# Six of the last z-gradient blocks brought token-major by a transposing load instead of by TensorE

## Chip, cores, metric

One core of a Trainium2 chip runs the whole program. The metric is the device time of one execution in microseconds (us). Three executions of the kernel before were timed; their median is the number that the kernel after is compared with. A fourth one, profiled, gives the trace.

## What is computed

The reference is the forward pass and the gradient of two alternating blocks, each used twice on a sequence of 2048 tokens with 512 columns. A is a long convolution (q times a filtered product of k and v), B is a dense layer with GELU. What matters here is the gradient of B's weights, summed over its two uses (layers 3 and 1):

```python
def _B_ref(x, w1, b1, w2, b2):
    h = jnp.einsum("bsd,df->bsf", x, w1) + b1
    h = _gelu(h)
    return jnp.einsum("bsf,fd->bsd", h, w2) + b2
```

With z the input of the GELU and gz its gradient (2048 tokens by F = 1376), the gradient of w1 is x^T gz (512 by 1376) and that of b1 is the sum of gz over the tokens. Both are summed over the two layers. The gradient of w2 is h^T g, with g the gradient that comes into the block.

## The kernel before

F is cut into NFC = 11 blocks of 128 columns (the last has 96). `weight_grads` (L1980) goes through 44 **units**, listed by `weight_grad_units` (L1970): a unit is one block c of one layer i. Units 0 to 21 (`which` = 0) make the gradient of w2 from h, units 22 to 43 (`which` = 1) that of w1 from gz. From unit 26 on the two layers of a block are neighbours: an even unit and the odd one after it sum into one PSUM tile `dw_ps`. Units 42 and 43 are the 96-column block.

A unit needs its 128 by 2048 block **token-major** (tokens on the partitions) as 16 weights of 128 by 128 in a tile `dw_tm`. Units 0 to 21 get it by a transposing load from DRAM (L2005). Units 22 to 43 load it feature-major (`dw_fm`, L2008), four units ahead; `turn_half` (L2010) then turns it on TensorE in two halves: eight transposes against the identity into one PSUM tile `dw_tp` (two buffers, shared with `dw_pt`), which ScalarE (ACT) copies to `dw_tm` (L2020). The halves of unit k+1 are issued in unit k before products 2 and 9. In unit 41, which has two successors in the tail, unit 43's halves come before products 5 and 13 (L2105).

`sum_rows` (L2023) sums the feature-major tile over the tokens for b1, then gives the tile back. It runs on ACT (L2027) while `m.sum_on_act` is set, else on VectorE (DVE, L2029). It stands before product 12 of unit k for unit k+1. `turn_out` (L2032) turns a finished block (`dw_pt`) in the second unit after it, `flush` (L2053) stores it.

The tail (L2077 to L2097) is the 96-column block. It goes the other way round: for each of four column blocks `dc`, 32 products of 96 columns (16 per layer), then an ACT copy (L2095) and a store of 192-byte rows. Before the third column block `sum_out` (L2042) turns the b1 sums.

Tiles come from seven tags; `take` (L1991) hands out the one that has been free longest, `give` returns one. A load on the SP queue into a tag waits for the tag's last reader, and everything behind it on SP waits too.

**Order of the work.** `weight_grads` is a generator that fills the gaps of `conv_backward` (the gradient of A): the latter yields the time it can spare, and products are issued until that is used up. A product counts 0.23, a half turn 0.45. TensorE, DVE and SP keep this program order. The stages of `conv_backward` from unit 33 on are, for each of four column blocks `cc`, 57 products `gh_ps` whose PSUM tiles (two buffers) ACT copies to `Wh` (L1265, L1269), then vector work, and between the second and the third 16 rows of `gk_ps`. Each `gh` stage yields 7.0:

```python
            yield 7.0
            state.sum_on_act = False
            if cc == 1:
                yield from k_rows()
```

so that sums go to ACT until the first `gh` stage has been covered. When `conv_backward` is through, the rest of the generator runs on its own. By these numbers and by the trace, the first `gh` stage lies in unit 33, the second in unit 34, the third in unit 38, the fourth in unit 39; what is left after that is unit 40, unit 41 and the tail.

Of the kernel before, what the change touches and what calls it, by code (L numbers as in the profile page):

```python
# [1349 lines left out]
def tok(ap2d, s):  # L1350
    return ap2d[s * 512:(s + 1) * 512, :].rearrange("(t p) d -> p t d", p=P)
# [625 lines left out]
    return units  # L1977


def weight_grads(nc, m, dims, aps, d):  # L1980


    D, F, S, ND, NFC, NT = dims.D, dims.F, dims.S, dims.ND, dims.NFC, dims.NT
    out7, out8, out9, out10 = aps["out_7"], aps["out_8"], aps["out_9"], aps["out_10"]
    b1a = d.evp.tile([P, 2, NFC], F32, name="b1a", tag="b1a", bufs=1)
    layers = (3, 1)
    units = weight_grad_units(NFC)
    fms, tms, pss, turned, late = {}, {}, {}, [], []
    spare, held = [f"dw_t{x}" for x in (0, 1, 2, 4, 5, 3, 6)], {}

    def take(name, key):  # L1991
        tag = held[key] = spare.pop(0)
        pool = d.evp if tag in ("dw_t3", "dw_t6") else d.tp if tag == "dw_t5" else d.share
        return pool.tile([P, S], BF16, name=name, tag=tag, bufs=1)

    def give(key):
        spare.append(held.pop(key))

    def fetch(k, sync):
        if k >= len(units):  # L2000
            return
        which, i, c = units[k]
        if which == 0:
            tms[k] = take("dw_tm", ("tm", k))[:, :].rearrange("p (t f) -> p t f", t=NT)
            sync.dma_start_transpose(out=tms[k], in_=m.h_d[layers[i]][:, c, :])  # L2005
        else:
            fms[k] = take("dw_fm", ("fm", k))
            sync.dma_start(out=fms[k], in_=m.gz_d[layers[i]][:, c, :])  # L2008

    def turn_half(k, half):  # L2010
        if k >= len(units) or not units[k][0]:
            return 0.0
        if half == 0:
            tms[k] = take("dw_tm", ("tm", k))[:, :].rearrange("p (t f) -> p t f", t=NT)
        ps = d.pp.tile([P, 8, P], BF16, name="dw_tp", tag="dw_tp")
        for j in range(8):
            t = 8 * half + j
            nc.tensor.transpose(out=ps[:, j, :], in_=fms[k][:, t * P:(t + 1) * P], identity=m.ident)
        dst = tms[k][:, 8 * half:8 * half + 8, :]
        nc.scalar.activation(out=dst, in_=ps, func=ACT.Identity)  # L2020
        return 0.45

    def sum_rows(k):  # L2023
        if k < len(units) and units[k][0]:
            which, i, c = units[k]
            if m.sum_on_act:
                nc.scalar.activation(out=fms[k], in_=fms[k], func=ACT.Identity, accum_out=b1a[:, i, c:c + 1])  # L2027
            else:
                nc.vector.tensor_reduce(out=b1a[:, i, c:c + 1], in_=fms[k], op=ALU.add, axis=mybir.AxisListType.X)  # L2029
            give(("fm", k))  # L2030

    def turn_out():  # L2032
        for o, f0, fcs in turned:
            pt = d.pp.tile([P, ND, P], F32, name="dw_pt", tag="dw_tp")
            for dc in range(ND):
                nc.tensor.matmul(pt[:, dc, :], lhsT=o[:, dc * P:(dc + 1) * P], rhs=m.ident, start=True, stop=True)
            oT = d.evp.tile([P, ND, P], BF16, name="dw_oT", tag="dw_oT")
            nc.scalar.activation(out=oT, in_=pt, func=ACT.Identity)
            late.append((oT[:, :, 0:fcs], out7[:, f0:f0 + fcs].rearrange("(c p) f -> p c f", p=P)))
        turned.clear()  # L2040

    def sum_out():  # L2042
        b1o = d.evp.tile([P, NFC], BF16, name="b1o", tag="b1o", bufs=1)
        nc.vector.tensor_tensor(out=b1o, in0=b1a[:, 0, :], in1=b1a[:, 1, :], op=ALU.add)
        pb = d.pp.tile([NFC, P], BF16, name="b1_ps", tag="dw_tp")
        nc.tensor.transpose(out=pb, in_=b1o, identity=m.ident)
        b1r = d.evp.tile([NFC, P], BF16, name="b1r", tag="b1r", bufs=1)
        nc.vector.tensor_copy(out=b1r, in_=pb)
        nfull = F // P
        late.append((b1r[0:nfull, :], out8[0:nfull * P].rearrange("(c p) -> c p", p=P)))  # L2050
        late.append((b1r[nfull:NFC, 0:F - nfull * P], out8[nfull * P:F].rearrange("(o p) -> o p", o=1)))

    def flush():  # L2053
        for o, ap in late:
            nc.sync.dma_start(out=ap, in_=o)
        late.clear()

    def reload(x, l):
        for s in range(4):
            nc.sync.dma_start(out=m.G[x][:, s * TS:(s + 1) * TS, :], in_=tok(m.n_d[l], s))  # L2060

    for k in m.early:
        held["tm", k] = spare.pop(0)
        tms[k] = m.early[k]
    fetched = 5
    for k in range(len(m.early), fetched):
        fetch(k, nc.sync)
    yield 0.01
    last = []
    for k, (which, i, c) in enumerate(units):  # L2070
        if which == 1 and units[k - 1][0] == 0:
            reload(1, 1)
        while fetched < len(units) and fetched <= k + (4 if units[fetched][0] else 5):
            fetch(fetched, nc.sync)
            fetched += 1
        f0, fcs = dims.FC[c]
        if which and c == NFC - 1:  # L2077
            last.append(tms.pop(k))
            if i == 0:
                continue  # L2080
            ps = d.pp.tile([P, ND, P], F32, name="dw_ps", tag="dw_ps")
            o = d.evp.tile([P, ND, P], BF16, name="dw_oT", tag="dw_oT")
            for dc in range(ND):
                for i in range(2):
                    for t in range(NT):
                        if (dc, i, t) == (0, 0, 7):
                            turn_out()
                        if (dc, i, t) == (2, 0, 0):
                            sum_out()
                        if (dc, i, t) == (3, 0, 0):  # L2090
                            flush()
                        nc.tensor.matmul(ps[:, dc, 0:fcs], lhsT=m.G[i][:, t, dc * P:(dc + 1) * P], rhs=last[i][:, t, 0:fcs],
                                         start=(i == 0 and t == 0), stop=(i == 1 and t == NT - 1))
                        yield 0.05
                nc.scalar.activation(out=o[:, dc, 0:fcs], in_=ps[:, dc, 0:fcs], func=ACT.Identity)  # L2095
                nc.sync.dma_start(out=out7[dc * P:(dc + 1) * P, f0:f0 + fcs], in_=o[:, dc, 0:fcs])
            continue  # L2097
        if i == 0:
            pss[c] = d.pp.tile([P, D], F32, name="dw_ps", tag="dw_tp" if which == 0 and c in (2, 3) else "dw_ps")
        ps, tm = pss[c], tms.pop(k)  # L2100
        for t in range(NT):
            if t in (2, 9):
                if turn_half(k + 1, int(t == 9)):
                    yield 0.45
            if k == len(units) - 3 and t in (5, 13):  # L2105
                yield turn_half(k + 2, int(t == 13))
            if t == 7:
                turn_out()
            if t == 12:
                flush()  # L2110
                sum_rows(k + 1)
            if k == len(units) - 3 and t == 15:
                sum_rows(k + 2)
            nc.tensor.matmul(ps, lhsT=tm[:, t, :], rhs=m.G[i][:, t, :], start=(i == 0 and t == 0),
                             stop=(i == 1 and t == NT - 1))
            yield 0.23
        give(("tm", k))
        if which == 0 and i == 0 and c == NFC - 1:
            reload(0, 3)
        if i == 0:  # L2120
            continue
        o = d.evp.tile([P, D], BF16, name="dw_o", tag="dw_o")
        nc.scalar.activation(out=o, in_=ps, func=ACT.Identity)  # L2123
        if which == 0:
            late.append((o[0:fcs, :], out9[f0:f0 + fcs, :]))
            if c == NFC - 1:
                b2o = d.evp.tile([P, D], BF16, name="b2o", tag="b2o", bufs=2)[fcs:fcs + 1, :]
                nc.scalar.activation(out=b2o, in_=ps[fcs:fcs + 1, :], func=ACT.Identity, scale=1.0 / PAD_H)
                late.append((b2o, out10.rearrange("(o d) -> o d", o=1)))
        else:  # L2130
            turned.append((o, f0, fcs))
    turn_out()
    flush()
# [301 lines left out]
```

## Time and profile before

| | us |
|---|---|
| median of 3 runs | 780.03 (779.84 to 780.92) |
| the profiled execution | 779.15 |
| its span, from first to last instruction | 776.9 |
| TensorE (PE) busy in the span | 743.0 (96%) |
| VectorE (DVE) busy | 705.6 (91%) |
| ScalarE (ACT) busy | 584.7 (75%) |
| GpSimd (POOL) busy | 222.8 (29%) |

The profiled execution takes 2.25 us more than its span, for what lies before the first and after the last instruction. In the trace's rows a matmul is one of TensorE's instructions and its weight load (PEld) another; line 56 is a helper through which every ordered instruction is recorded, so tiles tell them apart. In brackets stands the idle time before a row and what ended it.

### The profile page before, as it was taken

What the parts mean: (1) busy time and instruction counts of PE and PEld (TensorE: products, weight loads), DVE (VectorE), ACT (ScalarE), POOL (GpSimd) and SP (SyncE); (2) the same over time, 40 slices, a digit from 0 to 9 for tenths busy, and PEclk for the clock granted to TensorE, in tenths of its full rate; (3) what the DMA queues carried; (4) which work ended last, traced back from release to release, by engine and by line L of the source; (5) the groups of instructions that cost most, each with busy time, mean ns of one, the idle gap of its engine ahead of it and who ended that gap; (6) DMA issues with size and microseconds to landing.
All of it is one profiled execution on the core that took longest, in us unless ns stands there. A gap on an engine that the chain in (4) does not pass through costs nothing. (4 is left out here: it accounts for less than half of the span.)

```text
span 776.9 us, 13847 instructions
## 1 busy us (share of the span) xinstructions
PE 743.0 (96%) x5263; PEld 457.3 (59%) x5263; DVE 705.6 (91%) x1146; ACT 584.7 (75%) x792; POOL 222.8 (29%) x308
## 2 busy tenths in 40 slices
PE   8999899989999999999999999989999999999994
PEld 6765345655666666766666566434444465567764
DVE  8997999999999999999999989975999999999381
ACT  6999887799999999999788855445232199976662
POOL 6534520011233455254443342310012133020100
PEclk9999999999999999999999999999999999999998
DMA  9978888635571555779787978999999997755321
GB/s 313 332 287 308 298 317 293 119 89 136 161 215 49 168 144 167 209 206 216 217 249 205 254 181 239 235 312 248 255 269 193 375 390 278 252 154 170 116 76 26
DMA packets 199288, 169.39 MB, mean 218 GB/s; under 512 B 94195, under 2 KB 178870, under 8 KB 199094
## 3 DMA queue, kind: packets, MB, share of 16 engines
q1 hardware_dynamic: 186006, 127.31, 59.0%
q0 software_dynamic: 13216, 41.20, 15.1%
q8 instruction: 41, 0.67, 0.4%
q14 instruction: 25, 0.20, 0.1%
HBM read 76.36 MB, written 76.36 MB: 197 GB/s over the span
## 5 line engine op out<-in xcount | busy, mean ns | idle before, releaser
L56 PEld LDWEIGHTS <-w_sb 128*128 128x128 bf16 x903 | 84.9, 98 | 35.4 <-DMA low<-low 4.6
L56 PEld LDWEIGHTS <-dw_tm 128*128 128x128 bf16 x672 | 62.8, 98 | 64.0 <-DMA dw_tm<-h_d 2.4
L56 PE MATMUL mm_ps<-low,w_sb 128*128 128x256 bf16 x660 | 86.8, 273 | 3.9 <-DMA low<-low 3.9
L56 PE MATMUL dw_ps<-G,dw_tm 128*128 128x512 bf16 x336 | 82.6, 379 | 2.0 <-DMA dw_tm<-h_d 1.9
L56 PE MATMUL dw_ps<-x_sl,dw_tm 128*128 128x512 bf16 x336 | 81.8, 379 | 0.0
L56 PEld LDWEIGHTS <-w2T_sb 128*128 128x128 bf16 x704 | 68.9, 98 | 16.4 <-issue 1.0
L56 POOL TENSOR_TENSOR rstd<-rstd,mhalf 128x2 f32<-128x2 f32 (+1 forms) x28 | 36.3, 1296 | 98.0 <-DVE rstd L56 96.7
L56 PE MATMUL mm_ps<-W,w2T_sb 128*128 128x256 bf16 x440 | 58.3, 272 | 0.5 <-ACT l_g L56 0.3
L56 ACT ACTIVATE l_g<-l_g 128x2816 bf16<-128x2816 bf16 x22 | 57.2, 2601 | 1.4 <-DVE l_g L56 1.3
L56 POOL TENSOR_SCALAR ibx<-ident,ib 128x128 bf16<-128x128 bf16 x32 | 33.3, 1044 | 84.6 <-DVE W L56 82.2
L2020 ACT ACTIVATE dw_tm<-dw_tp 128x1024 bf16<-128x1024 bf16 x44 | 45.0, 1024 | 13.9 <-PE dw_tp L56 13.1
L2123 ACT ACTIVATE dw_o<-dw_ps 128x512 bf16<-128x512 f32 x21 | 12.5, 594 | 42.7 <-PE dw_ps L56 30.9
L56 PEld LDWEIGHTS <-ib 128*128 128x128 bf16 x264 | 25.6, 98 | 27.9 <-DVE ib L56 1.0
L56 DVE SCALAR_TENSOR_TENSOR gw_junk<-gy_bf,kTc 128x1024 bf16<-128x1024 bf16 x32 | 39.2, 1225 | 2.2 <-ACT gy_bf L1176 1.1
L56 ACT ACTIVATE l_n<-l_n,ib 128x512 bf16<-128x512 bf16 x32 | 25.5, 827 | 13.3 <-POOL ib L56 8.2
L56 PE MATMUL oo_ps<-w1T_sb,ib 128*128 128x512 bf16 x154 | 35.0, 379 | 0.0
L56 PE MATMUL mm_ps<-lane_t,w2T_sb 128*128 128x256 bf16 x264 | 34.0, 273 | 0.0
L56 ACT ACTIVATE W<-W 128x2816 bf16<-128x2816 bf16 x12 | 31.7, 2642 | 0.0
L56 ACT ACTIVATE low<-x_sl,nmr,rstd 128x512 bf16<-128x512 bf16 x36 | 30.2, 870 | 1.8 <-DVE nmr L56 1.8
L56 PE MATMUL oo_ps<-w_sb,l_h 128*128 128x512 bf16 x132 | 30.5, 379 | 0.5 <-DVE l_h L56 0.5
L56 ACT ACTIVATE ibx<-mm_ps 128x512 bf16<-128x512 f32 (+1 forms) x36 | 20.2, 577 | 14.2 <-PE mm_ps L56 14.1
L56 DVE TENSOR_TENSOR l_g<-l_g,l_g 128x2816 bf16<-128x2816 bf16 x19 | 30.7, 1614 | 0.0
(381 smaller groups left out, 1960.6 us busy)
## 6 DMA issues: line engine op xcount, KB each, us to landing
dw_fm<-gz_d SPq DMA_DIRECT2D x22, 512.0 KB, 10.7
l_n<-n_d SPq DMA_DIRECT2D x26, 256.0 KB, 3.7
gz_d<-ib SPq DMA_DIRECT2D x7, 704.0 KB, 5.1
W<-gp_d SPq DMA_DIRECT2D x7, 704.0 KB, 6.5
n_d<-low SPq DMA_DIRECT2D x18, 256.0 KB, 2.6
h_d<-l_h SPq DMA_DIRECT2D x6, 704.0 KB, 5.4
gz_d<-ibx SPq DMA_DIRECT2D x6, 704.0 KB, 4.8
KVspec_d<-KVg SPq DMA_DIRECT2D x4, 1024.0 KB, 6.4
```

What stands on the lines that cost most here:

```text
L56: return self.tc.keep_in_program_order(f(*args, **kwargs))
L2020: nc.scalar.activation(out=dst, in_=ps, func=ACT.Identity)
L2123: nc.scalar.activation(out=o, in_=ps, func=ACT.Identity)
```

## The change

Units 34, 36, 38, 40, 42 and 43 get their token-major tile by a transposing load from DRAM, issued on SP at the start of the unit three before, right after the feature-major load of the unit four ahead. They are not turned on TensorE and not copied by ACT. Their feature-major tile is still loaded, for the b1 sum; that sum is issued one unit earlier than it was, so that two sums stand together in units 32, 34, 36, 38 and 40, and unit 43's stands in unit 41 before product 12.

```diff
+TURNED_BY_LOAD = (34, 36, 38, 40, 42, 43)
...
+    def fetch_turned(k, sync):
+        if k in TURNED_BY_LOAD:
+            which, i, c = units[k]
+            tms[k] = take("dw_tm", ("tm", k))[:, :].rearrange("p (t f) -> p t f", t=NT)
+            sync.dma_start_transpose(out=tms[k], in_=m.gz_d[layers[i]][:, c, :])
+
     def turn_half(k, half):
-        if k >= len(units) or not units[k][0]:
+        if k >= len(units) or not units[k][0] or k in TURNED_BY_LOAD:
             return 0.0
...
             fetched += 1
+        fetch_turned(k + 3, nc.sync)
...
             if k == len(units) - 3 and t in (5, 13):
-                yield turn_half(k + 2, int(t == 13))
+                if turn_half(k + 2, int(t == 13)):
+                    yield 0.45
...
                 flush()
-                sum_rows(k + 1)
-            if k == len(units) - 3 and t == 15:
+                if k + 1 not in TURNED_BY_LOAD:
+                    sum_rows(k + 1)
+                if k + 2 in TURNED_BY_LOAD:
+                    sum_rows(k + 2)
+            if k == len(units) - 3 and t == 15 and k + 2 not in TURNED_BY_LOAD:
                 sum_rows(k + 2)
```

## Rows read from the trace of the kernel before

**Rows 1.** The page: busy us, share, instructions by engine; the instruction queue's packets, MB, share.

```profile
PE 743.0 (96%) x5263; PEld 457.3 (59%) x5263; DVE 705.6 (91%) x1146; ACT 584.7 (75%) x792; POOL 222.8 (29%) x308
...
q8 instruction: 41, 0.67, 0.4%
```

**Rows 2.** Stretches of the span: busy us (instructions) of PE, PEld, DVE, ACT, POOL; granted clock, DMA share, GB/s.

```profile
680.00:700.00 20.00, 18.47 (x153) 13.45 (x151) 19.29 (x30) 14.99 (x27) 4.11 (x3) 1.00 0.52 152
...
765.00:771.00 6.00, 0.37 (x9) 0.26 (x7) 0.00 (x0) 0.01 (x1) 0.00 (x0) 0.93 0.00 0
771.00:775.00 4.00, 2.72 (x32) 2.50 (x31) 0.00 (x0) 0.49 (x2) 0.00 (x0) 0.50 0.19 40
```

**Rows 3.** The chain of work that ended last, two pieces: start, us, what.

```profile
702.49 0.45 PE dw_tp L56 x8
...
763.80 7.17 another core or an unknown queue
```

**Rows 4.** The instructions in order of time, 677 to 696 us, ACT and TensorE.

```profile
677.73 1.90 ACT L2027 ACTIVATE dw_fm<-dw_fm 128x2048 bf16<-128x2048 bf16 x1
...
679.76 1.02 ACT L2020 ACTIVATE dw_tm<-dw_tp 128x1024 bf16<-128x1024 bf16 x1
680.68 1.09 ACT L1265 ACTIVATE Wh<-gh_ps 128x514 bf16<-128x514 f32 x2
681.33 5.50 PE L56 MATMUL gh_ps<-tabG,GY 128*128 128x257 bf16 x48 [1.18 <-ACT Wh L1265]
...
689.75 1.90 ACT L2027 ACTIVATE dw_fm<-dw_fm 128x2048 bf16<-128x2048 bf16 x1
...
691.64 0.59 ACT L2123 ACTIVATE dw_o<-dw_ps 128x512 bf16<-128x512 f32 x1
...
692.28 0.23 PEld L56 LDWEIGHTS <-dw_o 128*128 128x128 bf16 x4 [0.52 <-ACT dw_o L2123]
...
693.84 1.02 ACT L2020 ACTIVATE dw_tm<-dw_tp 128x1024 bf16<-128x1024 bf16 x1 [0.21 <-PE dw_tp L56]
694.07 0.38 PE L56 MATMUL gh_ps<-tabG,GY 128*128 128x257 bf16 x2
...
695.47 4.74 PE L56 MATMUL gh_ps<-tabG,GY 128*128 128x257 bf16 x41 [0.25 <-ACT Wh L1265]
```

**Rows 5.** The token-major tile: the transposing loads' issue time on SP in ns; landing in us.

```profile
L56 SPq DMA_TRANSPOSE dw_tm<-h_d x22: 2065/4222/12769, 478.6 to 598.1; - x22
...
DMA to landing us min/median/max: 4.6/7.5/10.1
```

**Rows 6.** The instructions in order of time, the tail from 759 us, TensorE and one ACT copy.

```profile
759.07 0.46 PE L56 MATMUL dw_ps<-dw_tm,G 128*128 128x96 bf16 x7
760.19 0.40 PE L56 MATMUL dw_pt<-ident,dw_o 128*128 128x128 bf16 x4 [0.66 <-ACT dw_o L2123]
...
763.85 0.84 PE L56 MATMUL dw_ps<-dw_tm,G 128*128 128x96 bf16 x16 [0.19 <-ACT dw_oT L2095]
764.52 0.84 PE L56 MATMUL dw_ps<-dw_tm,x_sl 128*128 128x96 bf16 x16
...
770.99 0.25 ACT L2095 ACTIVATE dw_oT<-dw_ps 128x96 bf16<-128x96 f32 x1 [7.19 <-remote]
...
771.29 1.44 PE L56 MATMUL dw_ps<-dw_tm,G 128*128 128x96 bf16 x16 [5.92 <-ACT dw_oT L2095]
772.53 1.48 PE L56 MATMUL dw_ps<-dw_tm,x_sl 128*128 128x96 bf16 x16
```

**Rows 7.** The DMA queues from 762 to 768 us: packets, MB, share of 16 engines.

```profile
DMA packets 289, 0.07 MB, mean 11 GB/s; under 512 B 288, under 2 KB 288, under 8 KB 288
...
q8 instruction: 1, 0.02, 3.1%
```

**Rows 8.** The waits, 8 to 757 us: us in total, times, longest.

```profile
PE mm_ps L56 <- DMA low<-low: 3.9, 2, 2.3
```

**Rows 9.** The last stores of the convolution's gradient, POOL, in order of time.

```profile
755.75 0.53 POOL L1287 DMA_DIRECT2D out_dram<-gh  x1 [13.21 <-DVE gdo L56]
```

## The prediction

> **What bounds the kernel.** I read the page first: TensorE is busy for 96% of the span, DVE for 91%, ACT for 75% [rows 1]. Next the stretches: from 680 us on TensorE still has 18.5 of 20 us, while the DMA engines are down to half their time [rows 2]. So work taken off TensorE there is worth its time, and DMA has room to take it. The chain of waits then shows two things that the shares hide. It runs through the turned halves, at 0.45 us a piece [rows 3], and it ends in 7.17 us "another core or an unknown queue". The timeline of the tail shows what that is: TensorE finishes the third column block at 765.36, its release reaches ACT only at 770.99, and TensorE starts again at 771.29 after 5.92 us without work [rows 6]. The timeline from 677 to 696 us shows that ACT is the second bound here: TensorE waits for ACT's `Wh` copies 1.18 us in the first `gh` stage and 0.25 us in the second, and 0.52 us for `dw_o` in unit 34, each behind a sum of the b1 gradient or the copy of a turned half [rows 4].
>
> **The sum, part by part.** (1) *Turning.* Six units have 12 halves; at 0.45 us [rows 3] TensorE loses 5.4 us of work. All of it is on the path: the `gh` stages lie at fixed amounts of counted work, a half (0.45) being replaced there by two products (0.46), so the saving shows after the fourth `gh` stage, where unit 40, unit 41 and the tail shrink to 7 products, unit 41 and the tail. -5.4.
>
> (2) *Waits behind unit 34's sum.* Now 1.90 us of ACT at 689.75 stand ahead of `dw_o` [rows 4]. That sum moves to unit 32, so the wait of 0.52 goes. -0.5.
>
> (3) *First `gh` stage.* In unit 32 two sums (33 and 34) now follow each other on ACT. Ahead of the first `Wh` copy a sum, one slot of 2.03 us (677.73 to 679.76), takes the place of a copy, one slot of 0.92 (679.76 to 680.68) [rows 4]. TensorE's wait of 1.18 grows to 2.3. +1.1.
>
> (4) *Second `gh` stage.* Here the change costs most. Sums 35 and 36 both come before product 12 of unit 34. By the counted work the first `gh` stage's 7.0 is not yet used up there (13 products of unit 33, then 12 products and two halves of unit 34, at 0.23 and 0.45, make 6.65), so both go to ACT, where before 35 went to DVE. TensorE reaches the stage at 694.07, plus 1.1 and less 0.9 for the two halves of 34, less 0.5 of (2), plus 0.7 for three more products: about 694.4. Two groups take it 1.15 us (694.07 to 695.22), to 695.6. ACT copies unit 35's second half (at about 693.5, 0.92), then makes two sums of 1.95 (2.03 and 1.89 in the rows), and only then copies `Wh`, 0.65 until TensorE resumes: 699.0 [rows 4]. A wait of 3.4 us in place of 0.25. Bounds: 0 if ACT took the copy first, 4.1 if both sums count in full. I take +3.1, by the row of the first stage, where ACT kept exactly this order.
>
> (5) *Start of the tail.* `dw_o` no longer queues behind unit 43's copy; of the 0.66 us wait [rows 6] I take off 0.2.
>
> (6) *The loads.* Six transposing loads of 512 KB are new. They landed in 7.5 us, 10.1 at most, and held SP 2.1 to 12.8 us each [rows 5]. Every one has three units of work ahead of its use, more than 13 us; the shortest is 43's, which waits on SP for unit 38's last product and is used after units 39, 40, 41 and the fourth `gh` stage (48 products at 0.23, two halves, 57 products at 5.50/48 = 0.115 [rows 4]): 18.5 us. Worst case by the rows is 12.8 + 10.1 = 22.9, late by 4.4; the median leaves 11. I take 0. Behind a waiting load on SP stand feature-major loads, due a unit or more later, and stores that nothing reads. DVE's sums 39 and 40 now wait for their loads and push the second `gh` stage's vector work back a few us; its result goes to a store only. The last such store was issued at 755.75 [rows 9]; it moves to about 759 and lands long before the end. Sums 41 to 43 now stand ahead of the last vector work, so `sum_out` waits for no sum.
>
> So far -5.4 - 0.5 + 1.1 + 3.1 - 0.2 = -1.9 us.
>
> The Trainium skill (VectorE: DVE Perf Modes, Rules for kernel authors) speaks against the change: turn 128 by 128 on TensorE where PSUM will do, at 390 ns against 1309 ns by DMA. An estimate from that page is 16 blocks x 1.309 = 21 us a unit, which would bring 43 late by some 2.5 us. The rows have 7.5 us for all 16 blocks and the measurement decides.
>
> (7) *The 5.92 us hole in the tail* is larger than all this. 41 packets of the instruction queue serve 10,526 TensorE instructions [rows 1], about 257 each (an estimate). One of them moves just before the hole [rows 7], and it is slow: 3.1% of 16 engines in 6 us is 3.0 us, against 0.4% of 16 x 776.9 us / 41 = 1.2 us in the mean [rows 1]. It moves among two stores of 192-byte rows, 288 packets under 512 bytes [rows 7]. In the tail a product takes under 50 ns (32 in 1.51 us, 763.85 to 765.36 [rows 6]), so whatever is late in instructions shows there and is covered elsewhere. The change removes 12 x 8 x 2 = 192 instructions, three quarters of a packet. Only 64 follow the hole, so the last call falls beyond the end, and the call before it comes to lie 257 - 192 = 65 instructions ahead of the old place: between the second and the third column block, its packet moving while the first block is computed, before any of those small stores. Bounds: the hole stays (0, and 1.2 more, since the third block too would run at the half clock that followed the hole: granted 0.50, 1.2 of 2.4 GHz, after 771 [rows 2], 2.72 us for a block in place of 1.51 [rows 6]); or it goes, -5.6 (a usual wait for ACT of some 0.3 remains) and -1.2. Forty other packets left no hole in the chain, and this one's company is gone, so I take the second.
>
> The Trainium skill (Runtime: NRT & Kernel Launch, Instruction fetch mechanics) says that the next block is fetched while the current one runs and that a crossing is mostly hidden. By that rule the hole is an exception and the time is the forecast's; by the row as it stands, it is the first rival's.
>
> **Total.** 776.9 - 1.9 - 5.6 - 1.2 = 768.2 us of span. The profiled execution took 779.15, 2.25 more than its span, and the median is another 0.88 above: **771.4 us**.
>
> **Rivals.** *The hole stays, one block earlier:* 776.9 - 1.9 + 1.2, on the median 779.4. For it: the tail's pace is the same, and that a fetch is the cause is inferred from one packet. Against it: the packet's slowness goes with its neighbours.
> *Slower: the wait for the two sums costs the clock.* TensorE's longest earlier wait was 2.3 us [rows 8] and cost none; 5.9 us did [rows 2, 6]. The new wait of 3.4 lies between. If the clock falls, the 48 products left of that `gh` stage take twice 0.115: +5.5. With the hole in place that is 784.9, without it 776.9; so it decides the sign if the hole stays.
> *ACT does not hold TensorE,* because sums and copies go another way round: parts (3) and (4) cost nothing and the sum is -6.1: 767.2, or 775 with the hole.
> *Loads come late* (the bounds of (6)): 43 by 4.4 us, 775.8, or 783.8 with the hole. The page on VectorE named under (6) would lead here too.
> *The change does nothing* would need the halves to be off the path; the chain names them.
>
> **Chances.** Forecast 0.48; hole stays 0.29; clock lost 0.08; ACT holds nothing 0.07; loads late 0.08. The range runs from 768.8 to 780.8: it takes the forecast, the first rival and the mixed cases, and leaves out the slow ends and the best one. The forecast's own range is 769 to 774. A measurement here can tell about 0.2%, 1.6 us. Faster: 0.48 + 0.07 + half of clock and loads + a little of the first rival, 0.62. Within it: most of the first rival, 0.25. Slower: 0.13.
>
> **What would show it.** Right: 256 of the 22 x 16 transposes left and 32 copies of turned halves; TensorE idle about 3.4 us at the second `gh` stage, released by `Wh`, behind two sums; the chain without an unknown piece, the tail's four column blocks about 1.9 us apart, the clock at 1.00 to the end. Wrong: an idle of 5 us between the second and third column block (first rival); a wait of TensorE or DVE for `dw_tm<-gz_d` or `dw_fm`; a granted clock under 1.00 near 697 us.

## The result and the profile after

The change made the kernel slower: 793.6 us median of six runs, against 782.0 for the kernel before beside it, a ratio on record of 1.0137 (95% interval 1.0104 to 1.0171; the two medians divided give 1.0149). The forecast was 771.4, with 768.8 to 780.8 as its range. The profiled execution took 791.14 us, its span 789.1, against 779.15 and 776.9 before.

The first view is the page: the engines' busy time, and the instruction queue. They answer to [rows 1].

```profile
PE 736.0 (93%) x5089; PEld 452.9 (57%) x5167; DVE 702.3 (89%) x1144; ACT 576.7 (73%) x784; POOL 221.6 (28%) x308
...
q8 instruction: 40, 0.66, 0.3%
```

The work did go: TensorE has 96 weight loads fewer, 12 halves of 8 (5263 to 5167; some matmul records are missing after, so the loads are counted), and its busy time fell. Its share fell too, so it waits more than before. Where, is best seen by cutting the span at marks that both kernels have. Each time is read from the timeline or the chain:

| stretch | before | after | difference | forecast |
|---|---|---|---|---|
| start to the first copy of a turned half (code that is the same) | 619.7 | 623.0 | +3.3 | 0 |
| to the 48 products of the first `gh` stage | 61.6 | 70.7 | +9.0 | +1.1 |
| to those of the fourth `gh` stage | 62.2 | 62.9 | +0.8 | +2.6 |
| to the last row of products | 29.0 | 17.1 | -11.9 | -11.8 |
| to the end of the span | 4.4 | 15.4 | +11.0 | -0.6 |
| sum | 776.9 | 789.1 | +12.2 | -8.7 |

The forecast's column sorts its own steps into these stretches: (3); (2) and (4); (1), (5), the hole of (7) and 0.6 of its 1.2 for the half clock (the hole's last block began in the fourth stretch); the other 0.6. The fourth row came as forecast, the second and the last cost 20 us between them. (The first row is not put down to the change: over the thirteen kernels profiled for this text that mark lies between 619.7 and 629.8.)

**The second row** is in ACT's part of the timeline, and in TensorE's beside it (start, us, instruction; in brackets the idle time before it and what ended it):

```profile
677.06 1.91 ACT L2036 ACTIVATE dw_fm<-dw_fm 128x2048 bf16<-128x2048 bf16 x1 [6.52 <-DMA dw_fm<-gz_d]
...
678.97 1.01 ACT L2029 ACTIVATE dw_tm<-dw_tp 128x1024 bf16<-128x1024 bf16 x1
```

```profile
680.03 0.61 PE L56 MATMUL dw_ps<-x_sl,dw_tm 128*128 128x512 bf16 x1 [5.63 <-ACT dw_tm L2029]
...
693.67 5.50 PE L56 MATMUL gh_ps<-tabG,GY 128*128 128x257 bf16 x48 [2.02 <-ACT Wh L1265]
...
708.32 5.50 PE L56 MATMUL gh_ps<-tabG,GY 128*128 128x257 bf16 x48 [1.21 <-ACT Wh L1265]
```

ACT stood 6.52 us at a sum of b1 whose feature-major tile was not there yet. That is unit 34's sum, and it had been put ahead of the copy of unit 31's second half, two units before its own place. TensorE then waited 5.63 us for that copy, with the tile's transposed blocks long done. The chain (start, us, what) names the load, 14.14 us from issue to landing, and the stretch behind it, shown last, ran at half clock:

```profile
662.90 14.14 DMA dw_fm<-gz_d
677.06 2.00 ACT dw_fm L2036 x2
```

```profile
679.00:686.00 7.00, 5.75 (x26) 3.23 (x28) 6.79 (x14) 7.00 (x9) 0.00 (x0) 0.51 0.35 75
```

(The last three numbers of a stretch are the granted clock, the DMA share and GB/s: 0.51 is the 1.2 GHz level.) The wait of 5.63, half of the 5.9 us that TensorE worked at that level (680.03 to 685.9) and the `gh` wait that grew from 1.18 to 2.02 [rows 4] make 9.4, a little over the stretch's 9.0.

**The last rows** are in the tail's timeline, which answers to [rows 6], POOL's stores, which answer to [rows 9], SP's waits (us in total, times, longest) and the DMA issues from 758 to 775 us (KB, median us to landing). An issue whose landing the trace doesn't tell is left out of the median; the last line is the issue of 771.16 by itself:

```profile
769.32 0.84 PE L56 MATMUL dw_ps<-dw_tm,G 128*128 128x96 bf16 x16 [0.34 <-ACT dw_oT L2105]
...
771.18 0.84 PE L56 MATMUL dw_ps<-dw_tm,G 128*128 128x96 bf16 x16 [0.19 <-ACT dw_oT L2105]
...
773.04 0.84 PE L56 MATMUL dw_ps<-dw_tm,G 128*128 128x96 bf16 x16 [0.34 <-ACT dw_oT L2105]
773.72 0.84 PE L56 MATMUL dw_ps<-dw_tm,x_sl 128*128 128x96 bf16 x16
```

```profile
769.50 0.53 POOL L1287 DMA_DIRECT2D out_dram<-gh  x1 [13.94 <-DVE b1o L56]
770.02 0.76 POOL L1289 DMA_DIRECT2D out_dram<-gdo  x1
```

```profile
SPq L2444 <- DMA out_dram<-gdo: 10.3, 1, 10.3
```

```profile
out_dram<-dw_oT SPq DMA_DIRECT2D x4, 24.0 KB, 14.3
out_dram<-gdo POOLq DMA_DIRECT2D x1, 1.0 KB, 16.6
...
out_dram<-dw_oT SPq DMA_DIRECT2D x1, 24.0 KB, 15.9
```

The hole is gone: four column blocks 1.86 us apart, where before one lay behind 5.92 us of nothing. But the kernel no longer ends with them. It ends with `gdo`, 512 sums of 2 bytes each, stored one element at a time (L1289). It is issued at 770.02 and lands 16.6 us later, at 786.6, when TensorE has been done for 12 us. The 24 KB store issued 0.7 us ahead of it (769.30) lands in 1.6 us; those issued behind it, at 771.16 and 773.01, need 15.9 and 14.3 us and land just after it. Before, `gdo` went out at 756.28, right behind the store of [rows 9]. The store issued at 761.96 needed 11.6 us, the one at 774.32 again 1.5, and their median is

```profile
out_dram<-dw_oT SPq DMA_DIRECT2D x4, 24.0 KB, 6.6
```

The views of the kernel before give no landing for `gdo`; the last mark of it in the trace is at 772.88, again 16.6 us after the issue.

### The profile page after: what moved, and what is told of

Its sections match the earlier page's. It is cut to its first block, busy times and chain, and to the rows that moved or that the text cites. A ratio compares the mean times of both kernels' runs of the same rounds, so it can differ in the third digit from the quotient of the medians.

```text
span 789.1 us, 13570 instructions
## 1 busy us (share of the span) xinstructions
PE 736.0 (93%) x5089; PEld 452.9 (57%) x5167; DVE 702.3 (89%) x1144; ACT 576.7 (73%) x784; POOL 221.6 (28%) x308
## 5 line engine op out<-in xcount | busy, mean ns | idle before, releaser
L56 PE MATMUL dw_ps<-x_sl,dw_tm 128*128 128x512 bf16 x325 | 79.7, 384 | 6.5 <-ACT dw_tm L2029 5.6
L56 PE MATMUL dw_ps<-G,dw_tm 128*128 128x512 bf16 x321 | 80.5, 381 | 2.5 <-DMA dw_tm<-h_d 1.8
L2029 ACT ACTIVATE dw_tm<-dw_tp 128x1024 bf16<-128x1024 bf16 x32 | 32.6, 1023 | 6.0 <-PE dw_tp L56 5.5
L56 DVE TENSOR_REDUCE b1a<-dw_fm 128x1 f32<-128x2048 bf16 x10 | 22.6, 2279 | 9.4 <-DMA dw_fm<-gz_d 9.4
```

Of the source, the lines that this page charges most:

```text
L56: return self.tc.keep_in_program_order(f(*args, **kwargs))
```

## The experiments

All stand against the kernel before, run on the same chip in turn; where no interval is given, the kernel ran once. Two theories came from this profile. *The order:* ACT's sum runs too early because nothing holds it. *The store:* the scattered `gdo` needs some 16 us and slows what is issued behind it; after, it sets the end, and before, it made the hole. Its rival is the forecast's reading, that the hole hangs on where an instruction packet falls.

**ACT in the written order.** The Ordered wrapper, which keeps an engine's instructions in the order of the text, covered TensorE, DVE and SP for the weight gradients, not ACT.

```diff
-            fill = weight_grads(Ordered(nc, tc, ("tensor", "vector", "sync")), m, dims, aps, dw)
+            fill = weight_grads(Ordered(nc, tc, ("tensor", "vector", "scalar", "sync")), m, dims, aps, dw)
```

> The kernel after, with ACT's instructions of the weight gradients kept in the order in which they are written, so that unit 34's sum stays behind unit 31's second copy. If the moved sum is what stops TensorE in unit 31, the idle of 5.6 us before unit 31's product 8 and the 6.8 us at half clock behind it (3.4 us lost) go, and the ratio to the kernel before falls from 1.014 to about 1.003 (some 9 us less than after). If the idle there is the load's own lateness (the rival), the sum still holds ACT for some us, now in unit 32, and less than 4 us is gained. Either way the end still waits for the store of the column sums gdo: TensorE's last product to the end of the span 12 us or more, as in the kernel after.

Measured: 785.05 us, ratio 1.006 (1.0038 to 1.0082). The stall in unit 31 is gone, with its half clock, and ACT waits for no feature-major tile any more, so the load was in time for the sum's own place. The `gh` stages then show what the forecast had worked out for this order (TensorE's timeline; then the stretch behind the second wait, its clock third from the right):

```profile
684.15 5.51 PE L56 MATMUL gh_ps<-tabG,GY 128*128 128x257 bf16 x48 [2.02 <-ACT Wh L1265]
...
700.69 7.14 PE L56 MATMUL gh_ps<-tabG,GY 128*128 128x257 bf16 x48 [3.10 <-ACT Wh L1265]
```

```profile
701.00:704.00 3.00, 3.00 (x17) 2.10 (x16) 3.00 (x6) 0.74 (x3) 0.60 (x1) 0.51 1.53 198
```

Waits of 2.02 and 3.10 us, forecast 2.3 and 3.4; and after the 3.10 the clock fell, which made the 48 products 7.14 us long in place of 5.50. So some 6 us were gained, not 9: in the kernel after, a sum that ran early no longer stood ahead of the second stage (1.21 us there), and in order it does: that stretch of the table is 66.4 us here, 3.5 more than after. The end is as it was, 13 us behind TensorE (SP's waits at the end):

```profile
SPq L2444 <- DMA out_dram<-gdo: 10.1, 1, 10.1
```

**`gdo` as four rows of 256 bytes,** in the kernel after, in the kernel before, and with ACT in order:

```diff
-            dma(out=out6.rearrange("(c p) -> p c", p=P), in_=gdo)
+        pg = d.pp.tile([ND, P], BF16, name="gdo_ps", tag="dw_tp")
+        nc.tensor.transpose(out=pg, in_=m.gdo, identity=m.ident)
+        gdr = d.evp.tile([ND, P], BF16, name="gdr", tag="gdr", bufs=1)
+        nc.scalar.activation(out=gdr, in_=pg, func=ACT.Identity)
+        nc.sync.dma_start(out=aps["out_6"].rearrange("(c p) -> c p", p=P), in_=gdr)
```

> The kernel after, with gdo turned on TensorE (two instructions) and stored by SP as 4 rows of 256 bytes in place of 512 elements of 2 bytes. If the scattered store is what ends the span and slows the other small stores, the last store lands within 4 us of TensorE's last product and the ratio falls from 1.014 to about 1.000 (some 10 to 11 us less). If small stores are slow by themselves at that point (the rival), the end stays 10 us or more behind TensorE's last product and the ratio at 1.01 or above. The stall of unit 31 stays, 5.6 us.

> The kernel before, with the same edit of gdo's store and nothing else. Theory: the scattered store, issued at 756 us, is what makes the 5.92 us hole between the third and fourth column block, by slowing the transfers around it (an instruction packet among them): the hole goes, ratio about 0.991 (7 us less). Rival, the prediction's: the hole belongs to the place of an instruction packet, 64 instructions before the end, which two more instructions hardly move: the hole stays at some 5 us, ratio 0.997 to 1.002.

> The kernel after with both edits. If the two causes are apart and both as supposed, their gains add up: ratio about 0.988 (9 us less in unit 31, 10 to 11 us less at the end, against a kernel after at 1.014), which would be below the kernel before and a little below the kernel before with gdo's rows (0.991). If only one holds, the ratio is that of its own run.

Measured: 1.0048 (1.0029 to 1.0068) after, 0.9969 (0.994 to 0.9998) before, 0.9987 (0.9967 to 1.0006) with ACT in order. In each the span ends within 4 us of TensorE's last product, and in the kernel before the hole is gone (0.34 us in its place); but each fell short of its number (1.000, 0.991 and 0.988). The list of waits gives a reason: one of 4.5 us that the kernel before has at 0.9, in code that was not touched (all three have this row). The third also has the wait of 3.10 us in the second `gh` stage, and its 48 products took 8.28 us.

```profile
PE iv_ps L56 <- DVE Yb L56: 4.5, 1, 4.5
```

The new tag `gdr` takes memory, so other tiles can move, and a DVE copy at 538 to 540 us (`spec_rb`), which had no wait in the kernel before, waits 12.2 us for TensorE, where the kernel before waits 8.6 a little later. So these three show the store's effect only beside that loss of 3.6 us (0.46%). The next run takes the small tile from a buffer that was there:

```diff
-        gdr = d.evp.tile([ND, P], BF16, name="gdr", tag="gdr", bufs=1)
+        gdr = d.evp.tile([P, D], BF16, name="gdr", tag="b2o", bufs=2)[0:ND, 0:P]
```

> The kernel before with gdo's rows stored as in the third run, but the small tile for them taken from an existing buffer, so that no other tile moves in memory. In the third run TensorE lost 4.5 us at 540 us to a product chain (iv_ps, behind DVE's Yb) that no other kernel loses there. If that loss came from the moved tiles, it goes back to 0.9 us, and the gain of the missing hole shows whole: ratio about 0.991 to 0.993. If the loss belongs to the new store, the ratio stays at 0.997.

Measured: 776.29 us, ratio 0.9941 (0.9918 to 0.9963), and the 4.5 us are gone, so they came with the tag and not with the store. The ratio lies just above the expected 0.991 to 0.993: the gain is 4.6 us (2.9 to 6.4), less than the 6.8 us that the hole and the half clock behind it took in the profile of before; whether the hole is as long in every execution no run shows. The tail of this run, and its DMA from 758 to 775 us (the queue's packets, MB and share; the stores):

```profile
768.17 0.84 PE L56 MATMUL dw_ps<-dw_tm,G 128*128 128x96 bf16 x16 [0.19 <-ACT dw_oT L2103]
...
770.03 0.50 PE L56 MATMUL dw_ps<-dw_tm,G 128*128 128x96 bf16 x8 [0.34 <-ACT dw_oT L2103]
```

```profile
q8 instruction: 1, 0.02, 0.3%
...
out_dram<-dw_oT SPq DMA_DIRECT2D x4, 24.0 KB, 1.5
```

The stores take 1.5 us, where the one issued behind the scattered `gdo` took 11.6, and the one instruction packet in this window 0.3% of 16 engines in 17 us, 0.8 us, where before it took 3.0 [rows 7].

**The store moved, TensorE untouched.** In the kernel before, `gdo` is copied by ACT and stored, still scattered, by SP at the last column block.

```diff
-            dma(out=out6.rearrange("(c p) -> p c", p=P), in_=gdo)
+        gdr = d.evp.tile([P, D], BF16, name="gdr", tag="b2o", bufs=2)[:, 0:ND]
+        nc.scalar.activation(out=gdr, in_=m.gdo, func=ACT.Identity)
+            nc.sync.dma_start(out=aps["out_6"].rearrange("(c p) -> p c", p=P), in_=gdr)
```

> The kernel before with the scattered store moved to the last column block of the tail (a copy of gdo on ACT, the store by SP), TensorE's instructions the same in number and order. If the store's company makes the hole, the hole of 5.92 us goes (a wait of about 0.3 in its place), TensorE's last product ends near 768, and the span ends where the store lands, 14 to 17 us after its issue, at some 783 to 787. If the hole hangs on the place of the instruction packet (the prediction's reading), it stays at some 5 us, since no TensorE instruction has moved.

Measured: 787.66 us beside 781.22. No TensorE instruction has moved, and the hole is gone; the span ends 16.8 us after TensorE's last row of products begins (768.70, span 785.5), waiting for the store, which lands 14.7 us after its issue at 769.6 (TensorE's timeline, and SP's waits):

```profile
768.02 0.84 PE L56 MATMUL dw_ps<-dw_tm,G 128*128 128x96 bf16 x16 [0.34 <-ACT dw_oT L2102]
```

```profile
SPq L2437 <- DMA out_dram<-gdr: 13.4, 1, 13.4
```

So the hole in the kernel before was this store's, and the packet's place by itself is ruled out as its cause. Whether the slowed packet was the link between the two was not tried, and the trace of before does not show it: from 766.5 to 771 us one packet moved, of under 512 bytes and not of the instruction queue, and TensorE still stood until 771.29; another instruction packet, from 685 us on, took 2.9 us and left no gap on TensorE.

**What makes the store slow.** Three runs, all with ACT in order: SP issues it; it is cut by columns, half early and half at the end; only half of the partitions are stored.

```diff
+            nc.sync.dma_start(out=out6.rearrange("(c p) -> p c", p=P), in_=gdo)
```

> The first run's kernel (ACT in order, gdo scattered) with the scattered store issued by SP in place of POOL. If it is the 512 elements of 2 bytes that make the store slow, it still lands some 14 to 18 us after its issue and the span still ends 10 us or more after TensorE's last product. If it is POOL's queue (the rival), the store lands in 2 to 4 us and the span ends within 4 us.

```diff
+            if cc in (1, 3):
+                    dma(out=out6.rearrange("(c p) -> p c", p=P)[:, cc - 1:cc + 1], in_=gdo[:, cc - 1:cc + 1])
```

> The first run's kernel (ACT in order, gdo scattered by POOL) with the scattered store cut in two: columns 0 and 1 go out after the second gh stage's vector work, columns 2 and 3 at the end. If the store's time goes with its elements of 2 bytes, the last one (256 of them) lands in about 8 us in place of 15.6, and the span ends 4 to 6 us after TensorE's last product in place of 13. If the time is a fixed one of such a store (the rival), it lands in 14 us or more and the end stays.

```diff
+            dma(out=out6.rearrange("(c p) -> p c", p=P)[0:64, :], in_=gdo[0:64, :])
```

> The first run's kernel (ACT in order, gdo scattered by POOL) with only the first 64 of the 128 partitions of gdo stored: 256 elements of 2 bytes, 64 in each of the four columns; the other half of that output is left out. Cutting the columns from four to two changed nothing (14.9 us). If the time goes with the elements of one column, which lie side by side in memory, the store lands in 7 to 9 us and the span ends 4 to 7 us after TensorE's last product. If it is fixed, 14 us or more and the end 12 us or more behind.

Measured from issue to landing: 16.6 us by SP (785.32 us in all beside 780.27), so POOL's queue is not the reason. For two columns 14.9 us (787.02 beside 781.22), where the theory that counts elements had 8, and 16.3 for the other two, issued at 740.0; for half of the partitions 12.6 (788.86 beside 785.17), between its two theories. The DMA issues of these two (the tail from 760 us on):

```profile
out_dram<-gdo POOLq DMA_DIRECT2D x1, 0.5 KB, 14.9
```

```profile
out_dram<-gdo POOLq DMA_DIRECT2D x1, 0.5 KB, 12.6
```

The time goes down with neither in proportion. Nor is it spent in moving the elements, as far as the trace records them: in the run with the moved store, issued at 769.6 and landed at 784.3, the DMA engines move their last packet before 771.5 (DMA packets, 771.5 to 784 us):

```profile
DMA packets 0, 0.00 MB, mean 0 GB/s; under 512 B 0, under 2 KB 0, under 8 KB 0
```

What the landing waits for in these 13 us stays open. The Trainium skill (DMA: Bandwidth & Descriptors, Rules for kernel authors) says that a non-contiguous last dimension becomes one descriptor per element and should be rearranged. The runs agree with the advice: as rows the same kilobyte no longer shows at the end. The limit of 512 bytes for full rate that the same page of the Trainium skill gives (Specifications) does not tell the two apart, since the rows of 192 bytes are below it too and took 1.5 us.

**Why the sum ran early.** All sums back at their old places in the text, ACT free:

```diff
-                if k + 1 not in TURNED_BY_LOAD:
-                    sum_rows(k + 1)
-                if k + 2 in TURNED_BY_LOAD:
-                    sum_rows(k + 2)
-            if k == len(units) - 3 and t == 15 and k + 2 not in TURNED_BY_LOAD:
+                sum_rows(k + 1)
+            if k == len(units) - 3 and t == 15:
```

> The kernel after with all sums of b1 written where the kernel before has them (product 12 of the unit ahead, so unit 34's stands in unit 33 again), ACT still free to be reordered. Theory A, the move of the sum in the text made it run early: the stall in unit 31 goes, about 9 us less than after. Theory B, what held the sum back in the kernel before were TensorE's turns, which read the tile that the sum overwrites, and without turns nothing holds it: the sum still runs ahead of unit 31's second copy, TensorE's stall in unit 31 is again 5 us or more with the half clock behind it.

Measured: 793.22 us beside 780.27, and the same stall, longer (the list of waits):

```profile
PE dw_ps L56 <- ACT dw_tm L2029: 6.3, 1, 6.3
```

So it was not the move in the text. The sum writes its tile in place, and TensorE's turns read that tile: in the kernel before a sum could not run until its unit's turns were done. Without turns it depends on its load alone, and on ACT nothing keeps it in its place. This is read from the program, and from the early sum in both kernels without these turns; no run held the sum by other means than the order, and why it came to stand just there is not shown.

**What is left of the change.** The kernel after with the sums at their old places, ACT in order, and `gdo` as rows from `b2o`'s buffer:

> The kernel after with three edits: the sums at their old places, ACT's instructions of the weight gradients kept in the written order, gdo stored as rows from the existing buffer. If the two causes found are all that stands against the change, what is left of it is the prediction's part (1), 5.4 us, less about 1 us for unit 35's sum, which the counted work now puts on ACT ahead of the second gh stage: 4 us below the kernel before with gdo's rows, ratio about 0.986. Waits of TensorE for Wh 1.2 us in the first stage and 1 to 1.5 in the second, the clock at full from 500 us to the end. If the loads themselves cost something (the rival), it is 0.991 or more.

Measured: 770.42 us, ratio 0.9859 (0.982 to 0.9898), the fastest of all, below both kernels and below the kernel before with the same rows (0.9941; the intervals don't meet). The clock is 0.998 over the whole span. The `gh` stages wait 0.25 and 1.21 us, at or under what was expected (TensorE's timeline):

```profile
689.31 5.51 PE L56 MATMUL gh_ps<-tabG,GY 128*128 128x257 bf16 x48 [0.25 <-ACT Wh L1265]
...
703.96 5.50 PE L56 MATMUL gh_ps<-tabG,GY 128*128 128x257 bf16 x48 [1.21 <-ACT Wh L1265]
```

Its profiled execution was its slowest (775.60), but in it the stretch from the fourth `gh` stage to the last row of products is 17.39 us (752.23 to 769.62), against 23.14 in the kernel before with rows (747.82 to 770.96): 5.75 less, 5.4 for the turns and 0.27 for `dw_o`.

## Why the prediction was wrong, point by point

(1) *Turning*: right in size and place. 5.4 us forecast, 5.75 less 0.27 measured between two kernels with the same store, behind the fourth `gh` stage.

(2) *Unit 34's wait*: it went; ACT copies `dw_o` at unit 33's end with no sum ahead of it (701.80, the moment it is there).

(3), (4) *The `gh` stages*: **the first step that failed.** Their premise, "ACT kept exactly this order", was read off one row of a kernel in which TensorE's turns held every sum back. The change took those turns away, and ACT was the one engine at work here that is not kept in order. As sizes they were good: with the order kept, 2.02 and 3.10 us for 2.3 and 3.4. As it was, 9.0 us were lost ahead of the first stage where 1.1 was forecast, and the second stage cost less than forecast. No rival had a sum that runs too early; the one in which sums and copies "go another way round" took it for a gain only.

*The clock's rival*: right in kind. The wait of 3.10 us came with a lower clock in all five kernels that had it, but at 1.3 to 2.8 us (1.64 in the first run), not 5.5, as the clock came back within the stage.

(5) *`dw_o` in the tail*: 0.39 us for 0.66, as forecast.

(6) *The loads*: TensorE never waited for one, as forecast. The trace tells the landing of two of the six only: 5.6 us, and 21.3, twice the rows' longest, for the one that held SP 13.74 us; the rows' own median and longest came from 8 of 22 loads. (An estimate from the Trainium skill, VectorE: DVE Perf Modes, The three transpose paths, stood at 21 us for each; in the last kernel above the two that are told took 5.0 and 5.8.) DVE did wait for feature-major tiles, 9.4 us in all. **The second step that failed is here**: of the last store of the convolution's gradient the text said "it moves to about 759 and lands long before the end". It moved to 769.50, `gdo` behind it to 770.02, and no price was asked for `gdo`. Most of that is the lateness of the whole kernel: the store of [rows 9] is issued 12.26 us after the fourth stage's 48 products begin before, and 12.92 after. What counts is the distance to the end: from `gdo`'s issue to the end of TensorE's last product it was 17.7 us and is 4.5. Of these 13.2 us, 5.7 are the saving of (1) and (5), which lies behind that stage as (1) had itself said, 6.8 the hole and its half clock, and 0.7 DVE's later sums. With the 16.6 us as its price, a `gdo` issued just behind the forecast's 759 would have landed near 776, past the 768.2 forecast for the span (an estimate from these numbers). What it cost: 11.0 us at the end in place of a gain of 0.6.

(7) *The hole*: gone, as forecast, and the fourth row of the table holds it (-11.9 for -11.8), but for another reason, so its size is right by luck. The text saw a slow packet among small stores and took the packet's place for the cause, and the stores of 192-byte rows for the company. The company was `gdo`. In the kernel after both have moved: the tail's instruction packet to 769.0, between the first and the second column block, about as forecast, and `gdo` to 770.02, behind it. The run with the moved store shows that moving `gdo` is enough; that the packet's move would have been enough is not tried. It would still have lain in the time from `gdo`'s issue at 756.28 to its last mark at 772.88. So one cause gave back the hole and took the end.

## What to carry to other kernels

When a change removes instructions, list what they held back: a write in place behind them is free to run as soon as its data are in, and on an engine that a scheduler may reorder it will block what stands behind it. A transfer's price has to be known before it is moved near the end, small stores above all: look at how long everything behind it takes, not at its kilobytes. And an unexplained hole should be tested by moving its suspected neighbours one at a time; here one moved store would have shown the price that decided the sign.

## What the runs showed of the hardware

- A store of 512 separate elements of 2 bytes took 14.7 to 16.6 us from issue to landing in five kernels, from POOL's queue or SP's, and 256 such elements 12.6 to 16.3. Stores of 24 KB issued behind it landed just after it, in up to 15.9 us; ahead of it, or without it, they took 1.5 to 2.4.
- What an idle TensorE costs in clock varied. Behind a wait of 2.02 us the 48 products of the `gh` stage took 5.5 us in six kernels and 7.14 in the run with the cut store; behind 3.10 us they took 6.79 to 8.28 in all five that had it; after 5.63 us the granted clock was 0.51 for seven us.
- A small tile with a tag of its own, 4 rows of 256 bytes, cost 3.6 us in a part of the kernel that has nothing to do with it; in a buffer that was there it cost none of this. That other tiles moved in memory is the likely reason, but was not looked at.
